# Three of four score blocks split for fp32r, six buffers for rows of scores, and a small copy moved to ScalarE

## The chip, the core and the metric

The kernel runs on one core of a Trainium2 chip. The metric is the device time of one execution in microseconds (us); the kernel before took 876.58 us (median of 3 runs, 874.64 to 881.66). The engines are named as the profile names them: PE (TensorE matmul) with PEld (its weight loads), DVE (VectorE), ACT (ScalarE), POOL (GpSimd), and SP, whose queue issues nearly all DMAs.

## What is computed

Attention with a mixing of the 12 heads ahead of the softmax and another behind it, then a two-matrix layer with a quadratic gate. The sizes are batch 4, 12 heads, 448 positions, 64 columns per head; 1792 tokens of 768, inner width 2048.

```python
scores = scale * q @ k.T
scores = einsum('bhij,hg->bgij', scores, w_pre)    # "first mixing"
attn = softmax(scores)
attn = einsum('bhij,hg->bgij', attn, w_post)       # "second mixing"
x = (attn @ v)  -> [1792, 768]
h = x @ w_in;  g = where(h >= 1, h, where(h <= -1, 0, (h + 1)**2 / 4))
out = g @ w_out
```

## The kernel before

The attention part takes about the first 430 us after a short start, the layer the rest. A *tile* is up to 120 query rows of one batch entry (three tiles of 120 and one of 88 per entry, 16 in all). Scores of a tile are made for all 12 heads and kept in SBUF as `ssb`, 120 rows by 12 heads by 448. For the first mixing heads and rows must lie together on the partitions, so `load_s` (L198) copies ten rows of `ssb`, with their twelve heads, by DMA into a buffer `s10` of 120 partitions by 448: that is a *block*. A tile of 120 rows has 12 blocks, one of 88 rows has 9; there are 180. A tile's blocks make three *groups* of 4 (or of 3), 48 groups in all.

The order of work is written out by hand: one *window* per group n in the main loop (from L880 on), and every engine runs its instructions in that order. In window n the program has

- on SP's queue, first the loads of s for group n+1 (L198), then loads of q, k, v and of layer weights, and stores;
- on PE `pre(m)` for the blocks 0, 1, 2, 3 of group n in that order (L217 or L219), transposes of q and k for a later tile, the products with v (`pv`, L302 and L307, into `ps_q`), the second mixing of group n-1 (L272, L256), and at the window's end a third of the scores of a later tile (`scores`, L180, the first half into the same `ps_q`, of which there is one);
- on DVE the row maxima of the four blocks (L222), one split of a block of group n+1 (L206, L207), a reciprocal (L235), low parts of transposed k and q (L146, L166), part of the copy of `pv`'s product into `xo` (L326), the other split, two steps of a weight conversion (L373, L374, in windows that have one), and the copy of the scores into `ssb` (L183);
- on ACT the exponentials (L228), then the copies of `pv` (L319) and of the second mixing (L258), and half of the scores (L185).

`pre` has two forms. A block that was *split* into a high and a low fp32r part (`split`, L201 to L208) is mixed by three matmuls (L217); one that was not is mixed in fp32 (L219), which the trace shows as two records per block. Before the change the blocks 1 and 3 of each group but the first are split (block 1 of a group of 3): 82 of 180. Their loads are issued first, so the order of loads is 1, 3, 0, 2. `s10` has 8 buffers, the high and low parts 2 each.

For a tile of 88 rows the copy into `xo` has a second piece of 2 by 18 columns (`full < nb`, L322 to L328): DVE does it for three of the four such tiles (9 copies), ACT for the last.

The first group of a tile can be loaded only after the last third of that tile's scores was copied into `ssb` (L183, L185), which happens two windows before the group is used. The convert-and-store of layer weights and the loads of v run in the same SP queue between the loads of s.

Of the kernel before, what the change touches and what calls it, by code (L numbers as in the profile page):

```python
# [9 lines left out]
F32 = mybir.dt.float32  # L10
F32R = mybir.dt.float32r
# [3 lines left out]
AF = mybir.ActivationFunctionType  # L15
# [7 lines left out]
def tile_talking_heads_moe(  # L23
# [11 lines left out]
    nc = tc.nc  # L35
    B, H, S, D = q.shape
# [5 lines left out]
    KM = IB * H  # L42
# [16 lines left out]
    ap_ = s_att.enter_context(tc.tile_pool(name="att", bufs=2))  # L59
# [14 lines left out]
    tiles = []  # L74
    for b in range(B):
        for i0 in range(0, S, QT):
            n = min(QT, S - i0)
            tiles.append((b, i0, n, -(-n // IB)))
    blocks = []
    groups = []  # L80
# [6 lines left out]
    NG = len(groups)  # L87
# [99 lines left out]
    s10 = {}  # L187
# [6 lines left out]
    def load_s(m):  # L194
        t, o, ni, c = blocks[m]
        n, nb = tiles[t][2:]
        x = ap_.tile([KM, S], F32, tag="s10", name="s10", bufs=8)
        nc.sync.dma_start(out=x[:ni * H], in_=ssb[t][o:n:nb])  # L198
        s10[m] = x

    def split(m):  # L201
        k = blocks[m][2] * H
        x = s10.pop(m)
        hi = ap_.tile([KM, S], F32R, tag="sh", name="sh", bufs=2)
        lo = ap_.tile([KM, S], F32R, tag="sl", name="sl", bufs=2)
        nc.vector.tensor_copy(out=hi[:k], in_=x[:k])  # L206
        nc.vector.tensor_tensor(out=lo[:k], in0=x[:k], in1=hi[:k].bitcast(F32), op=ALU.subtract)  # L207
        s10[m] = (hi, lo)  # L208

    def pre(m):  # L210

        k = blocks[m][2] * H
        lps[m] = ps_l.tile([KM, S], F32, tag="l", name="ps_l")
        x = s10.pop(m)
        if isinstance(x, tuple):
            for j, (w, y) in enumerate(((wpre_h, x[0]), (wpre_l, x[0]), (wpre_h, x[1]))):
                nc.tensor.matmul(out=lps[m], lhsT=w[:k], rhs=y[:k], start=(j == 0), stop=(j == 2))  # L217
        else:
            nc.tensor.matmul(out=lps[m], lhsT=wpre[:k], rhs=x[:k], start=True, stop=True)  # L219

    def row_max(m, nm):
        nc.vector.tensor_reduce(out=nm, in_=lps[m], axis=AX.X, op=ALU.max, negate=True)  # L222
        lps[m] = (lps[m], nm)
# [24 lines left out]
    def post(m):  # L248
        t, o, ni, c = blocks[m]
        a = place(t)[0]  # L250
        ps = ps_l.tile([128, KC, H * IB], F32, tag="l", name="ps_a")
        e, w = ex[m], wr[m]
        for r in range(KC):
            for s in ((0, 1), (1, 0))[r % 2]:
                c0 = r * 128 + s * 64
                nc.tensor.matmul(out=ps[half[s], r, :ni * H], lhsT=e[:, c0:c0 + 64], rhs=w[:, :, :ni],  # L256
                                 start=True, stop=True)
        nc.scalar.activation(out=a[:, :, :, c:c + ni],  # L258
                             in_=ps[:, :, :ni * H].rearrange("q r (h i) -> q r h i", h=H), func=AF.Copy)
# [23 lines left out]
    def banks_x(n):  # L283
        if n < NG - 4:
            x = pair()
        elif n < NG:
            x = bank(0)
        else:
            return [ps_l.tile([128, QT], F32, tag="l", name="ps_x") for m in range(2)]
        return [x[:, :, :QT]]  # L290

    def pv(t, g, step):
        b, i0, n, nb = tiles[t]
        if g == 0:
            xo[t] = ap_.tile([128, HP, QT], F32, tag="xo", name="xo", bufs=2)
        ps = banks_x(step)
        to = [ps[0][:, m, :] for m in range(2)] if len(ps) == 1 else ps
        a, ar = aT[t]
        x, xr = vt[b, g]
        for s in range(2):  # L300
            for m, p in enumerate(half):
                nc.tensor.matmul(out=to[m][half[s], :n], lhsT=xr[p, s, :], rhs=ar[p, 2 * g + s, :n],  # L302
                                 start=True, stop=False)
        for m in range(2):
            for r in range(KC):
                for s in ((0, 1), (1, 0))[r % 2]:
                    nc.tensor.matmul(out=to[m][half[s], :n], lhsT=x[:, 2 * m + s, r * D:(r + 1) * D],  # L307
                                     rhs=a[:, r, 4 * g + 2 * m + s, :n], start=False, stop=(r == KC - 1))

        full = n - (IB - 1) * nb  # L310

        def out():
            for i, p in enumerate(ps):
                to = xo[t][:, 2 * g:2 * g + 2, :nb * IB]
                if len(ps) == 2:
                    to = to[:, i:i + 1]
                    p = p.unsqueeze(1)
                to = to.rearrange("p m (a o) -> p m a o", o=nb)
                nc.scalar.activation(out=to[:, :, :, :full],  # L319
                                     in_=p[:, :, :full * IB].rearrange("p m (o a) -> p m a o", a=IB),  # L320
                                     func=AF.Copy)
                if full < nb:  # L322
                    x = to[:, :, :IB - 1, full:]
                    y = p[:, :, full * IB:n].rearrange("p m (o a) -> p m a o", a=IB - 1)
                    if t + 1 < len(tiles):
                        nc.vector.tensor_copy(out=x, in_=y)  # L326
                    else:
                        nc.scalar.activation(out=x, in_=y, func=AF.Copy)  # L328
        return out

    def visit(n, rests):
        v = [lambda x=x: pv(*x, n) for x in vis2.pop(n, ())]
        if rests:
            v.insert(len(v) if n < NE else 0, lambda: post_rest(rests))
        return [f() for f in v]
# [46 lines left out]
    def conv(n, f):  # L382
        if n in CS and CS.index(n) < 2 * NF:
            f(CS.index(n))
# [372 lines left out]
    with tc.manual_schedule():  # L757
# [45 lines left out]
        for m in groups[0]:  # L803
# [7 lines left out]
            out=wpre.rearrange("p (i g) -> p i g", g=H),  # L811
# [3 lines left out]
            out=wpost, in0=wrep[:, 1, :].unsqueeze(2).to_broadcast([KM, H, IB]),  # L815
# [59 lines left out]
        def w0_lo():  # L875
            wts[0] = wts[0]()
            sum_x("B11", "B12", "B11", 0)
            sum_x("B12", "B22", "B12", 0)
# [11 lines left out]
        for n in range(NG + 2):  # L890
            if n == NE:
                s_qk.close()
                s_se.close()
                pool['w'] = ctx.enter_context(tc.tile_pool(name="ffw", bufs=2, side="right",
                                                           reuse_waits="tile"))
                pool['ps_h'] = ctx.enter_context(tc.tile_pool(
                    name="ps_h", bufs=1, space=PSUM, side="right", reuse_waits="tile"))
            if n == NG - 1:
                s_ss.close()
            ms = groups[n] if n < NG else ()  # L900
            old = list(groups[n - 1]) if 0 < n <= NG else []
            if n + 1 < NG:
                for m in (*groups[n + 1][1::2], *groups[n + 1][::2]):
                    load_s(m)
            for f in loads.get(n, ()):
                f()
            if ms:
                sm = ap_.tile([KM, 4], F32, tag="sm", name="sm", bufs=3)
                nm = ap_.tile([KM, 4], F32, tag="nm", name="nm", bufs=3)
            for m in ms:  # L910
                pre(m)
            nxt = list(groups[n + 1][1::2]) if n + 1 < NG else []
            turned = [f() for f in [f() for f in at.pop(n, ())]]
            for f in mid.pop(n, ()):
                f()
            conv(n + 1, conv_load)
            for m in ms:
                row_max(m, nm[:, m - ms[0]:m - ms[0] + 1])
            if n == NG - 1:
                w0_lo()  # L920
            if nxt:
                split(nxt.pop(0))
            rests = list(old)
            early = n < NE
            copies = visit(n, rests) if early else ()
            for j, m in enumerate(ms):
                if j == 3 and old and not early:
                    post(old.pop(0))
                exps(m, j, sm)
            conv(n, conv_scaled)  # L930
            if ms:
                norm(ms, sm)
            for f in (*turned, *copies):
                f()
            for m in nxt:
                split(m)
            if n == NG:
                step(0)
            for m in old:
                post(m)  # L940
            conv(n, conv_rest)
            conv(n - 1, conv_store)
            if not early:
                for f in visit(n, rests):
                    f()
            for t, hps in vis.pop(n, ()):
                scores(t, hps)
            for f in late.pop(n, ()):
                f()
# [155 lines left out]
```

## Time and profile before

| | us | share of the span |
|---|---|---|
| median of three runs | 876.58 (874.64 to 881.66) | |
| the profiled execution, device time | 878.23 | |
| its span in the profile | 876.5 | |
| PE busy | 854.6 | 97% |
| DVE busy | 644.6 | 74% |
| ACT busy | 563.5 | 64% |
| POOL busy | 213.9 | 24% |
| chain that ended last: PE | | 84% |
| chain that ended last: DMA | | 9% |

The profiled execution lies 1.7 us over its span and 1.65 us over the median. "Busy" of PE is modelled from starts, so idle PE is read from gaps and waits more safely than from the busy share. A wait is put down to what ended last. DMA share is the mean busy share of the core's 16 DMA engines.

### The profile page before, as it was taken

Reading aid. Unit: us, or ns where it says so; the run is one execution under the profiler, and the core shown is the slowest. Engines: PE = TensorE matmul, PEld = TensorE weight load, DVE = VectorE, ACT = ScalarE, POOL = GpSimd, SP = SyncE. Lnnn points to the kernel's source line nnn. Section 1 sums busy time; section 2 is a strip of 40 time slices with the busy share of each in tenths; the row PEclk is TensorE's granted clock in tenths of the full one; section 3 lists DMA queues with packets and bytes.
Section 4 is the critical chain, followed back from the end, with each engine's and each line's share of the span. In section 5 each row is a group of like instructions: output and inputs, shape, how many; then the busy total and the mean of one; then the engine's idle time right before and its main releaser. Section 6 shows DMA issues by size and latency. Waiting matters only on the chain.

```text
span 876.5 us, 19947 instructions
## 1 busy us (share of the span) xinstructions
PE 854.6 (97%) x7850; PEld 736.4 (84%) x7850; DVE 644.6 (74%) x945; ACT 563.5 (64%) x1162; POOL 213.9 (24%) x269
## 2 busy tenths in 40 slices
PE   8999999999998999989999999999999999999998
PEld 6678877778776778768778788899999999999998
DVE  3888577786766776867668877997668978777853
ACT  3688788787886778868776566676667534433431
POOL 0266235663355543656320000000000000000000
PEclk8999999999999999999999999999999999999999
DMA  7687769986699876988555745654444444123331
GB/s 160 209 239 236 207 186 264 267 257 196 170 255 253 249 210 172 278 261 260 180 182 169 265 150 172 224 189 133 129 116 162 154 171 135 55 84 115 107 128 63
DMA packets 155329, 162.47 MB, mean 185 GB/s; under 512 B 66916, under 2 KB 148964, under 8 KB 155236
## 3 DMA queue, kind: packets, MB, share of 16 engines
q1 hardware_dynamic: 152404, 160.51, 60.9%
q8 instruction: 62, 1.02, 0.5%
q10 hardware_dynamic: 2832, 0.69, 0.4%
q14 instruction: 31, 0.25, 0.1%
HBM read 88.81 MB, written 33.82 MB: 140 GB/s over the span
## 4 chain that ended last, share of the span: by engine, by line
PE 84%; DMA 9%; DVE 3%; ACT 2%; SPq 1%; issue 1%; ACTq 0%
PE ps_f L711 23%; PE ps_f L546 21%; PE ps_a L256 10%; PE ps_l L219 8%; PE ps_q L307 5%; PE ps_l L217 5%; DMA s<-ssb 4%; PE ps_q L180 3%; PE ps_s L180 3%; DMA v<-in_v_dram 2%; PE ps_r L272 2%; PE ps_q L302 1%; DMA k<-in_k_dram 1%; PE ps_k L141 1%; DMA wraw<-in_moe_w_in_dram 1%; PE ps_t L161 1%
## 5 line engine op out<-in xcount | busy, mean ns | idle before, releaser
L239 POOL TENSOR_SCALAR wr<-wpost,rs 120x120 f32<-120x120 f32 x180 | 142.1, 805 | 64.0 <-DVE rs L235 47.4
L228 ACT ACTIVATE e<-ps_l,nm 120x448 f32<-120x448 f32 x180 | 112.1, 631 | 55.6 <-DVE nm L222 54.5
L256 PE MATMUL ps_a<-wr,e 120*64 120x120 f32 (+1 forms) x2160 | 118.9, 266 | 0.0
L222 DVE TENSOR_REDUCE nm<-ps_l 120x1 f32<-120x448 f32 x180 | 105.0, 619 | 13.6 <-PE ps_l L219 10.4
L256 PEld LDWEIGHTS ps_a<-wr,e 120*64 120x64 f32 x2160 | 110.2, 137 | 2.6 <-issue 2.6
L694 ACT ACTIVATE sgh_p<-gq_p 128x1024 fp32r<-128x1024 f32 (+1 forms) x56 | 53.3, 953 | 90.5 <-PE ps_f L711 90.3
L438 DVE SCALAR_TENSOR_TENSOR wl<-wi,wh 128x768 fp32r<-128x768 f32 x71 | 67.7, 954 | 41.9 <-ACT wh L435 41.3
L711 PE MATMUL ps_f<-wh,sgh_p 128*128 128x384 f32 x294 | 98.2, 334 | 0.0
L711 PE MATMUL ps_f<-wh,sgl_p 128*128 128x384 f32 x294 | 98.2, 334 | 0.0
L711 PE MATMUL ps_f<-wl,sgh_p 128*128 128x384 f32 x294 | 98.2, 334 | 0.0
L435 ACT ACTIVATE wh<-wi 128x768 fp32r<-128x768 f32 x71 | 59.7, 842 | 58.7 <-DVE wi L658 18.0
L219 PE MATMUL ps_l<-s,wpre 120*120 120x448 f32 x196 | 93.7, 562 | 1.9 <-ACT ssb L185 1.1
L258 ACT ACTIVATE aT<-ps_a 128x360 f32<-128x360 f32 x180 | 79.9, 493 | 13.3 <-PE ps_a L256 4.7
L695 DVE TENSOR_TENSOR sgl_p<-gq_p,sgh_p 128x1024 fp32r<-128x1024 f32 (+1 forms) x56 | 60.9, 1089 | 35.7 <-ACT sgh_p L694 35.7
L206 DVE CAST sh<-s 120x448 fp32r<-120x448 f32 (+1 forms) x82 | 32.5, 396 | 59.4 <-DMA s<-ssb 59.4
L183 DVE COPY ssb<-ps_q 120x896 f32<-120x896 f32 (+1 forms) x48 | 52.1, 1085 | 29.6 <-PE ps_q L180 29.6
L185 ACT ACTIVATE ssb<-ps_s 120x448 f32<-120x448 f32 (+1 forms) x96 | 47.1, 544 | 28.7 <-PE ps_s L180 26.6
L376 POOL TENSOR_TENSOR wt<-wt,wk 128x768 int32<-128x768 int32 x32 | 58.2, 1820 | 6.7 <-ACT wk L372 6.7
L217 PE MATMUL ps_l<-sh,wpre_h 120*120 120x448 f32 (+1 forms) x82 | 58.7, 715 | 0.0
L711 PEld LDWEIGHTS ps_f<-wh,sgh_p 128*128 128x128 f32 x294 | 55.2, 188 | 0.0
L711 PEld LDWEIGHTS ps_f<-wl,sgh_p 128*128 128x128 f32 x294 | 55.2, 188 | 0.0
L711 PEld LDWEIGHTS ps_f<-wh,sgl_p 128*128 128x128 f32 x294 | 55.2, 188 | 0.0
(234 smaller groups left out, 1946.3 us busy)
## 6 DMA issues: line engine op xcount, KB each, us to landing
s<-ssb SPq DMA_DIRECT2D x172, 210.0 KB
wraw<-in_moe_w_in_dram SPq DMA_DIRECT2D x16, 768.0 KB
wraw<-in_moe_w_out_dram SPq DMA_DIRECT2D x16, 768.0 KB
wi<-wod SPq DMA_DIRECT2D x29, 384.0 KB
wi<-wsd SPq DMA_DIRECT2D x28, 384.0 KB
wsd<-wt SPq DMA_DIRECT2D x16, 384.0 KB
wod<-wt SPq DMA_DIRECT2D x16, 384.0 KB
wi<-wss SPq DMA_DIRECT2D x16, 384.0 KB
```

The costliest lines, as they stand in the source:

```text
L217: nc.tensor.matmul(out=lps[m], lhsT=w[:k], rhs=y[:k], start=(j == 0), stop=(j == 2))
L219: nc.tensor.matmul(out=lps[m], lhsT=wpre[:k], rhs=x[:k], start=True, stop=True)
L222: nc.vector.tensor_reduce(out=nm, in_=lps[m], axis=AX.X, op=ALU.max, negate=True)
L228: nc.scalar.activation(out=e, in_=ps, func=AF.Exp, bias=nm, accum_out=sm[:, j:j + 1])
L239: nc.gpsimd.tensor_scalar_mul(out=w[:, :, :ni], in0=wpost[:, :, :ni], scalar1=rs[:, j:j + 1])
L256: nc.tensor.matmul(out=ps[half[s], r, :ni * H], lhsT=e[:, c0:c0 + 64], rhs=w[:, :, :ni], start=True, stop=True)
L258: nc.scalar.activation(out=a[:, :, :, c:c + ni], in_=ps[:, :, :ni * H].rearrange("q r (h i) -> q r h i", h=H), func=AF.Copy)
L435: nc.scalar.activation(out=hi, in_=t, func=AF.Copy, scale=2.0 ** -8)
L438: nc.vector.scalar_tensor_tensor(out=lo, in0=t, scalar=2.0 ** -8, in1=hi.bitcast(F32), op0=ALU.mult, op1=ALU.subtract)
L546: nc.tensor.matmul(out=o, lhsT=u[:, c, k], rhs=x, start=first and r == 0 and m == 0, stop=r == 2 and m == 2, skip_group_check=True)
L695: nc.vector.tensor_tensor(out=lo, in0=src, in1=hi.bitcast(F32), op=ALU.subtract)
L711: nc.tensor.matmul(out=o, lhsT=x[:, f, c], rhs=y[:, f % 2, :], start=first and f == 0 and m == 0, stop=hf == 1 and f == 3 and m == 2, skip ...
```

## The change

All blocks of a group but block 0 are split (so 129 instead of 82 of the 180: 47 more, one more in each group but the first). The loads of a group come in the order 1, 2, 3, 0. The buffers for loaded rows go from 8 to 6, those for the high and low parts from 2 to 3 each, so the SBUF they take together is the same. The small second piece of the copy into `xo` is always done by ACT.

```diff
     def load_s(m):
-        x = ap_.tile([KM, S], F32, tag="s10", name="s10", bufs=8)
+        x = ap_.tile([KM, S], F32, tag="s10", name="s10", bufs=6)
     def split(m):
-        hi = ap_.tile([KM, S], F32R, tag="sh", name="sh", bufs=2)
-        lo = ap_.tile([KM, S], F32R, tag="sl", name="sl", bufs=2)
+        hi = ap_.tile([KM, S], F32R, tag="sh", name="sh", bufs=3)
+        lo = ap_.tile([KM, S], F32R, tag="sl", name="sl", bufs=3)
...
                     y = p[:, :, full * IB:n].rearrange("p m (o a) -> p m a o", a=IB - 1)
-                    if t + 1 < len(tiles):
-                        nc.vector.tensor_copy(out=x, in_=y)
-                    else:
-                        nc.scalar.activation(out=x, in_=y, func=AF.Copy)
+                    nc.scalar.activation(out=x, in_=y, func=AF.Copy)
...
             if n + 1 < NG:
-                for m in (*groups[n + 1][1::2], *groups[n + 1][::2]):
+                for m in (*groups[n + 1][1:], groups[n + 1][0]):
                     load_s(m)
...
-            nxt = list(groups[n + 1][1::2]) if n + 1 < NG else []
+            nxt = list(groups[n + 1][1:]) if n + 1 < NG else []
```

## Rows read from the trace of the kernel before

**Rows 1.** The page: busy time by engine, and the chain by engine.
```profile
PE 854.6 (97%) x7850; PEld 736.4 (84%) x7850; DVE 644.6 (74%) x945; ACT 563.5 (64%) x1162; POOL 213.9 (24%) x269
...
PE 84%; DMA 9%; DVE 3%; ACT 2%; SPq 1%; issue 1%; ACTq 0%
```

**Rows 2.** Windows view: start:end, length, busy us (count) by engine, clock, DMA share, GB/s.
```profile
27.30:72.60 45.30, 45.23 (x515) 33.93 (x515) 37.42 (x71) 37.37 (x98) 24.55 (x32) 1.00 0.82 234
72.60:120.00 47.40, 47.40 (x604) 37.57 (x604) 32.78 (x57) 36.65 (x90) 19.05 (x28) 1.00 0.74 208
120.00:192.00 72.00, 69.11 (x921) 54.86 (x921) 54.40 (x102) 57.50 (x144) 41.75 (x45) 1.00 0.87 258
192.00:231.00 39.00, 39.00 (x492) 30.77 (x489) 26.07 (x45) 29.66 (x73) 14.47 (x23) 1.00 0.67 191
231.00:306.00 75.00, 69.69 (x921) 54.71 (x921) 53.06 (x100) 56.53 (x144) 40.76 (x45) 1.00 0.88 246
306.00:345.00 39.00, 39.00 (x490) 30.68 (x486) 26.93 (x47) 29.31 (x73) 15.34 (x23) 1.00 0.69 194
345.00:418.00 73.00, 69.82 (x924) 55.17 (x923) 55.63 (x103) 58.13 (x145) 43.87 (x48) 1.00 0.85 258
418.00:456.00 38.00, 36.97 (x503) 28.59 (x502) 22.92 (x43) 27.31 (x73) 12.50 (x23) 1.00 0.55 183
```

**Rows 3.** Waits of the whole run: us in total, times, longest.
```profile
DVE sh L206 <- DMA s<-ssb: 59.4, 38, 4.4
PE ps_q L180 <- DVE xo L326: 9.5, 6, 2.3
```

**Rows 4.** Timeline of PE, first mixings of one group: start, us, instruction.
```profile
212.86 1.01 PE L219 MATMUL ps_l<-s,wpre 120*120 120x448 f32 x2
...
214.12 0.36 PE L217 MATMUL ps_l<-sl,wpre_h 120*120 120x448 f32 x1
214.32 0.91 PE L219 MATMUL ps_l<-s,wpre 120*120 120x448 f32 x2
```

**Rows 5.** Timeline of PE around 256 to 280.
```profile
266.28 0.46 PE L180 MATMUL ps_q<-kh,qh 64*120 64x448 f32 x2 [2.34 <-DVE xo L326]
267.69 1.01 PE L219 MATMUL ps_l<-s,wpre 120*120 120x448 f32 x2
...
276.45 0.46 PE L180 MATMUL ps_q<-kh,qh 64*120 64x448 f32 x2 [1.47 <-DVE xo L326]
278.28 0.98 PE L219 MATMUL ps_l<-s,wpre 120*120 120x448 f32 x2 [0.34 <-DMA s<-ssb]
```

**Rows 6.** Timeline of DVE around 264 to 280.
```profile
264.56 0.39 DVE L206 CAST sh<-s 120x448 fp32r<-120x448 f32 x1 [4.39 <-DMA s<-ssb]
264.98 0.63 DVE L207 TENSOR_TENSOR sl<-s,sh 120x448 fp32r<-120x448 f32 x1
265.52 0.17 DVE L235 RECIPROCAL rs<-rs 120x4 f32<-120x4 f32 x1
...
268.56 1.08 DVE L183 COPY ssb<-ps_q 120x896 f32<-120x896 f32 x1
...
275.17 0.39 DVE L206 CAST sh<-s 120x448 fp32r<-120x448 f32 x1 [3.41 <-DMA s<-ssb]
...
276.68 0.41 DVE L206 CAST sh<-s 120x448 fp32r<-120x448 f32 x1 [0.28 <-DMA s<-ssb]
```

**Rows 7.** Timeline of SP's queue, loads of s for two successive groups.
```profile
259.23 3.37 SPq L198 DMA_DIRECT2D s<-ssb  x4
...
267.55 4.46 SPq L198 DMA_DIRECT2D s<-ssb  x4
```

**Rows 8.** Chain in order of time, two places: start, us, what.
```profile
269.56 8.59 DMA s<-ssb
278.14 0.14 issue
...
391.14 8.22 DMA s<-ssb
399.36 0.14 issue
```

**Rows 9.** The tile xo: duration ns min/median/max, first and last start.
```profile
L326 DVE COPY xo<-ps_q x9: 170/191/194, 141.8 to 388.2; 128x36 f32<-128x36 f32 x9
L328 ACT ACTIVATE xo<-ps_x x6: 187/198/246, 466.6 to 468.3; 128x18 f32<-128x18 f32 x6
```

**Rows 10.** Windows view of a stretch in which loads of s move nearly alone.
```profile
122.00:125.00 3.00, 3.00 (x68) 2.84 (x66) 2.07 (x6) 2.97 (x9) 0.92 (x3) 1.00 0.65 243
```

**Rows 11.** Timeline of DVE at 192, where a long stretch of conversions ends.
```profile
192.22 1.08 DVE L183 COPY ssb<-ps_q 88x896 f32<-88x896 f32 x1
193.45 2.61 DVE L222 TENSOR_REDUCE nm<-ps_l 120x1 f32<-120x448 f32 x4 [0.15 <-PE ps_l L219]
```

## The prediction

> **What bounds the kernel now.** I read the page first. PE is busy for 854.6 of 876.5 us and carries 84% of the chain that ended last, DMA 9% and DVE 3% [rows 1]. A bound that looks like PE throughout has to be read by stretch, because all of the change lies in the attention part, 27 to 456 us, and because the sum over stretches hides who comes second. The windows view cut at the places where the DMA share changes shows two kinds [rows 2]. In four stretches (27 to 73, 120 to 192, 231 to 306, 345 to 418; 265 us together) the DMA engines are busy for 82 to 88% of the time; three of them are also the ones in which PE stands idle, 2.9, 5.3 and 3.2 us. In the four between (163 us together) the DMA share is 55 to 74% and PE is idle for 1.0 us in all: there PE sets the pace.
>
> Next the waits. PE's largest one in the attention part is the scores (L180) waiting for DVE's small copy of xo (L326): 9.5 us in six times; DVE waits 59.4 us in 38 times for loads of s in its splits [rows 3]. The timelines tie the two together. In the window that begins at 256, the loads of s for the next group are issued at 259.2 [rows 7]; DVE's first split stands until 264.56, 4.39 us idle, for the first of them [rows 6]; behind it on DVE queue the reciprocal, the copy L326 and the rest; PE's scores need the `ps_q` that L326 reads and start at 266.28 after 2.34 us of idleness [rows 5]. The window behind repeats it with 1.47 us. So the wait carries DVE's name, but a transfer is what is late.
>
> Last the chain in order of time, for what sets the beginning of a window inside such a stretch. PE begins the window at 278.28 after 0.34 us of waiting for a load of s [rows 5], and the chain has that load from 269.56 to 278.15 [rows 8]. It is the third of the four issued from 267.55 on [rows 7], and by the old order 1, 3, 0, 2 the third is block 0, the one that PE mixes first. The same pattern stands at 391.14 to 399.36 [rows 8]. The three landings of that group can be read off: 275.15 and 276.66 from DVE's two waiting casts [rows 6], 278.14 from PE. They are 1.5 us apart although three issues lie within 2.9 us: the transfers queue behind one another.
>
> **The change part by part.** *Splits on PE.* One block fewer in fp32, one more in three fp32r matmuls. By the modelled ends of one group's mixings, the fp32 pair ends at 213.87, the fp32r triple behind it at 214.48 and the next fp32 pair at 215.23 [rows 4]: 0.61 us against 0.75, so 0.14 us saved per block. Over 47 blocks this is 6.6 us, if PE set the pace in every window. It does so in the 163 us of the low-DMA stretches. A window takes (456 - 27.3)/48 = 8.9 us on average, so these are about 18 windows and 18 x 0.14 = 2.5 us. In the others the bytes that DMA has to move don't change, and what PE saves is waited for again; I take 0 there, and 4.1 us as the other end.
>
> *The order of loads.* Block 0 becomes the fourth load, and PE still needs it first. Where a window's beginning is held by the third load today, it will be held by the fourth. No row shows when the fourth lands. From below it is 0 (it lands before PE is through with the window anyway, as between the stretches), from above the 1.5 us at which the landings follow each other in rows 5 and 6; the pitch of four unhindered issues, 3.37/4 = 0.84 us [rows 7], lies between. I take 1.0. This doesn't add up from window to window as long as the transfers are what is late, because the landings then stay at their absolute times. It counts once at the end of each of the four stretches, where PE takes over again: 4 x 1.0 = 4.0 us, bounds 0 and 6.0.
>
> *The copy L326.* Moved to ACT it costs about 0.2 us (an ACT copy of half its size 0.198, L326 itself 0.191 on DVE [rows 9]), nine times, 1.8 us on an engine that is idle for 20 to 25% of these stretches [rows 2]; hidden. The six waits of 9.5 us disappear under that name. What is late next is the beginning of the following window: with scores done 2.3 us sooner, PE meets block 0, which is now the last load. At 278 today's order already gives PE only what was left after the wait of 1.47 us, and still a wait of 0.34 us for the third load. So I take 0 of the 9.5 us as kept; the other end is all of it.
>
> *Splits on DVE.* A split takes 0.96 us from its cast to the next instruction (264.56 to 265.52 [rows 6]), so 47 x 0.96 = 45 us more. In a stretch of 72 us with 8 windows DVE goes from 54.4 to 62.1 us, 86% [rows 2]. That fits, but the new split stands ahead of the copy of scores into `ssb` (L183), so this copy and the next row maxima come a split later. At 192, where a stretch of conversions ends, DVE was idle for only 0.15 us ahead of the row maxima [rows 11], so they will be late by up to 0.8 us there and the exponentials on ACT behind them; PE first has the other mixings and transposes to do, which covers about 0.5 of it. I take 0.3 us for each of the three places like this, 0.9 us, bounds 0 and 3 x 0.96 = 2.9. The later L183 also delays the loads of the first group of each tile. In a loaded stretch they queue anyway: at 259.23 they are issued and only at 264.5 does the first land [rows 6, 7]. I take 0.
>
> *The buffers.* The third and fourth load of a group now wait for the first and second split of the group before, the ones that free their buffers. Those splits end at 265.52 and about 267.1 [rows 6]; the third load of the group behind is issued at 269.56 [rows 8]. The buffer is free in time: 0. Where SP runs further ahead (the low-DMA stretches), a load that is held back for a microsecond or two has a whole window left; 0 there too.
>
> The sum: -2.5 + 4.0 + 0 + 0.9 = +2.4 us. Against the profiled execution (878.23, span 876.5) this gives 880.6, and on the median of the three runs 876.58 + 2.4 = 879.0.
>
> A rule and a row about whether the loaded stretches are really full. A DMA share of 85 to 88% [rows 2] reads like 12 to 15% of room, and then loads could land sooner, once engines ask sooner. But in a stretch in which loads of s move nearly alone the share is 0.65 with transfers queued behind each other [rows 10]. The Trainium skill ("DMA: Bandwidth & Descriptors", section "Why a DMA increments its semaphore by 16 and not by 1") says that a copy is spread over the largest number of engines, up to 16, that divides the slowest dimension on both sides. For ten rows of `ssb` into 120 partitions that would be ten of 16, an estimate of 0.63, and the trace's 0.65 agrees. By that rule 0.85 to 0.88 has little room left; by the share alone up to 9 us in the 72 would be free. It is why the first rival below gets no more than its chance.
>
> **The rivals.** *A: the stalls go for good.* If the fourth load lands before PE gets to the next window, the 9.5 us of waits for L326 and the 6.6 us of PE work are both kept: 876.6 - 16.1 = 860.5. With half of the waits kept and the low-DMA splits, about 8 us, it is 868. For it: the waits have DVE's name, and DVE in-order blocking is what the change removes. Against it: the third load already comes too late at 278 and 399 [rows 5, 8], and the fourth comes later. It decides where the fourth load lands within half a microsecond of the third.
>
> *B: the delay feeds itself; slower.* If what is late is the issue of the loads and not their bytes, a window that begins 1 us later copies its scores 1 us later, the next tile's loads start 1 us later, and the shift adds up. About 30 windows lie in the loaded stretches (265/8.9). A shift of 1.0 us kept in a third to a half of them is 10 to 15 us, with 2.5 saved: 884 to 889, and with a split's 0.96 us on DVE in each path up to 893. It decides from the point where the DMA queues run dry between two groups' loads. Against it: the spacing of 1.5 us of landings issued faster than that.
>
> *C: DVE becomes the bound.* 86% busy with waits for PE and DMA between may be full. If every one of some 24 windows with a conversion grows by 0.4 us, this is +10 us: 887. Against it: DVE's idle time is mostly the wait for s itself, 59.4 us [rows 3], which the work can move into.
>
> *D: the time stays and nothing is decided.* The split's saving and the later block 0 cancel to less than a microsecond: 876 to 878. It is the forecast with other roundings and shares its chance.
>
> **How the numbers follow.** About 1% (8.8 us) is what a measurement of this kernel can tell from no change. The forecast with D gets 0.70, its own range being 873 to 884 (the terms at their bounds: -2.5 - 4.1 + 0 at one end, about +6.0 + 2.9 - 2.5 at the other, rounded out by the run-to-run spread). A gets 0.12, B 0.13, C 0.05. Faster by over 1% is A: 0.12. Slower by over 1% is B and C: 0.18. Within 1%: 0.70. For 8 in 10 the range has to reach some way into A and over most of B: 866 to 890.
>
> **What would show it.** If the steps are right: the wait of PE for L326 is gone; in its place PE's first fp32 mixing of a window (L219) waits for loads of s in the loaded stretches, some 10 us in all; the low-DMA stretches are each 0.5 to 0.9 us shorter, the loaded ones about 1 us longer; DVE has 129 splits, 45 us more work, and waits less than 59 us for s. The prediction is wrong if PE has no such wait (then A), if SP waits longer for L183 and the DMA share falls in the loaded stretches (then B), or if PE waits for `ps_q` or for exponentials behind DVE without a load being late (then C).

## The result, and the profile after

The changed kernel took 883.88 us (median of 11 runs, 876.27 to 886.84), the kernel before 877.37 us in the same series (11 runs, 874.64 to 882.28). The ratio is 1.0062 with a 95% interval of 1.0038 to 1.0085: 5.4 us more, 3.3 to 7.5. (The two medians lie 6.5 us apart; the text goes by the ratio and its interval.) That is within 1%, and the sign is settled.

The profiled execution after took 884.98 us with a span of 883.2; that is 6.75 us over the profiled one of before. A profile shows one execution, and executions of one kernel lie several us apart (876.27 to 886.84 here), so the ratios decide and the profiles only explain. Its page, busy time by engine and the chain by engine, as in [rows 1]:

```profile
PE 852.0 (96%) x7897; PEld 747.2 (85%) x7897; DVE 688.1 (78%) x1030; ACT 558.7 (63%) x1171; POOL 218.6 (25%) x269
...
PE 68%; DVE 13%; DMA 10%; ACT 6%; issue 2%; SPq 0%; POOL 0%; ACTq 0%; DVEq 0%
```

DVE does 43.5 us more and is busy for 78% of the span, so nobody would call it the bound. The chain says more: PE's share fell from 84% to 68%, and DVE's rose from 3% to 13%, ACT's from 2% to 6% [rows 1]. DMA rose by one point only. DVE has come into the path that sets the end.

The windows view of after, cut at the beginnings of the same windows of the program as in [rows 2] (which lie later here), in the same columns:

```profile
27.30:75.50 48.20, 44.93 (x521) 34.97 (x520) 41.63 (x81) 36.51 (x97) 23.87 (x32) 1.00 0.73 221
75.50:123.80 48.30, 47.12 (x609) 38.51 (x609) 38.32 (x69) 36.27 (x91) 20.84 (x28) 1.00 0.73 204
123.80:200.30 76.50, 71.33 (x931) 58.15 (x929) 62.58 (x116) 57.80 (x147) 44.07 (x46) 0.96 0.83 246
200.30:238.40 38.10, 38.10 (x492) 31.43 (x491) 29.17 (x53) 29.06 (x73) 14.71 (x22) 1.00 0.66 188
238.40:312.30 73.90, 68.91 (x932) 56.40 (x930) 61.90 (x116) 56.47 (x147) 41.66 (x47) 1.00 0.85 251
312.30:350.30 38.00, 38.00 (x492) 31.42 (x490) 29.07 (x53) 28.86 (x73) 14.51 (x21) 1.00 0.69 196
350.30:424.90 74.60, 68.92 (x932) 56.45 (x930) 61.85 (x116) 55.54 (x147) 41.82 (x46) 1.00 0.82 250
424.90:462.60 37.70, 36.52 (x509) 29.73 (x508) 27.99 (x52) 27.11 (x74) 15.30 (x24) 1.00 0.58 189
```

Against [rows 2] the eight lengths changed by +2.9, +0.9, +4.5, -0.9, -1.1, -1.0, +1.6 and -0.3 us, together +6.6. The loaded stretches (the first, third, fifth and seventh) gave +7.9, but not alike: one of them became shorter. The stretches between gave -1.3. In the loaded stretches the DMA share fell from 0.82, 0.87, 0.88 and 0.85 to 0.73, 0.83, 0.85 and 0.82. In the third and seventh this is what the same bytes give over a longer time (0.87 x 72 / 76.5 = 0.82, 0.85 x 73 / 74.6 = 0.83); in the first and fifth it is lower than that.

Waits of the whole run after (us in total, times, longest), then those of SP's queue between 27 and 470 us:

```profile
ACT e L228 <- DVE nm L222: 81.3, 50, 4.2
...
DVE sh L206 <- DMA s<-ssb: 32.0, 32, 2.9
...
PE ps_l L219 <- DMA s<-ssb: 13.0, 11, 2.9
```

```profile
SPq L198 <- DVE ssb L183: 74.8, 24, 11.1
SPq L198 <- DVE sh L206: 12.8, 15, 2.5
```

PE's wait for the small copy into `xo` (9.5 us in [rows 3]) is gone; its wait of 13.0 us for a load of s stands in its place. DVE waits 27 us less for loads; part of the third split's work now fills that idleness. Two waits have grown that [rows 3] doesn't show: before, ACT's exponentials waited 54.5 us for row maxima, and SP waited 59.8 us for L183 (the copy of scores into `ssb`). Now they wait 81.3 and 74.8 us.

### The profile page after: what moved, and what is told of

Read it like the earlier page. It is cut to its first block, busy times and chain, and to the rows that moved or that the text cites. A ratio compares the mean times of both kernels' runs of the same rounds, so it can differ in the third digit from the quotient of the medians.

```text
span 883.2 us, 20160 instructions
## 1 busy us (share of the span) xinstructions
PE 852.0 (96%) x7897; PEld 747.2 (85%) x7897; DVE 688.1 (78%) x1030; ACT 558.7 (63%) x1171; POOL 218.6 (25%) x269
## 3 DMA queue, kind: packets, MB, share of 16 engines
q1 hardware_dynamic: 152404, 160.51, 59.8%
## 4 chain that ended last, share of the span: by engine, by line
PE 68%; DVE 13%; DMA 10%; ACT 6%; issue 2%; SPq 0%; POOL 0%; ACTq 0%; DVEq 0%
PE ps_f L708 23%; PE ps_f L543 21%; DMA s<-ssb 8%; PE ps_a L256 6%; PE ps_l L217 4%; ACT e L228 3%; PE ps_l L219 3%; PE ps_q L307 3%; DVE ssb L183 2%; PE ps_q L180 2%; DVE wt L371 2%; DVE sl L207 2%; DVE sh L206 2%; PE ps_s L180 2%; DVE wt L370 1%
## 5 line engine op out<-in xcount | busy, mean ns | idle before, releaser
L228 ACT ACTIVATE e<-ps_l,nm 120x448 f32<-120x448 f32 x180 | 112.0, 632 | 81.8 <-DVE nm L222 81.3
L239 POOL TENSOR_SCALAR wr<-wpost,rs 120x120 f32<-120x120 f32 x180 | 146.6, 830 | 37.3 <-DVE rs L235 30.8
L222 DVE TENSOR_REDUCE nm<-ps_l 120x1 f32<-120x448 f32 x180 | 103.1, 617 | 9.1 <-PE ps_l L219 7.7
L207 DVE TENSOR_TENSOR sl<-s,sh 120x448 fp32r<-120x448 f32 x129 | 82.0, 636 | 4.4
L206 DVE CAST sh<-s 120x448 fp32r<-120x448 f32 x129 | 52.0, 403 | 32.6 <-DMA s<-ssb 32.0
L219 PE MATMUL ps_l<-s,wpre 120*120 120x448 f32 x102 | 51.2, 589 | 17.0 <-DMA s<-ssb 13.0
L183 DVE COPY ssb<-ps_q 120x896 f32<-120x896 f32 (+1 forms) x48 | 52.1, 1085 | 17.0 <-PE ps_q L180 16.9
L217 PE MATMUL ps_l<-sh,wpre_h 120*120 120x448 f32 x129 | 64.4, 499 | 0.0
L185 ACT ACTIVATE ssb<-ps_s 120x448 f32<-120x448 f32 (+1 forms) x96 | 48.1, 569 | 16.5 <-PE ps_s L180 15.3
L234 POOL TENSOR_SCALAR rs<-sm 120x4 f32<-120x4 f32 (+1 forms) x48 | 12.6, 262 | 177.0 <-ACT e L228 177.0
```

What stands on the lines that cost most here:

```text
L183: nc.vector.tensor_copy(out=ssb[t][:n, h:h + 2, :], in_=wide[:n, :, :S])
L228: nc.scalar.activation(out=e, in_=ps, func=AF.Exp, bias=nm, accum_out=sm[:, j:j + 1])
L239: nc.gpsimd.tensor_scalar_mul(out=w[:, :, :ni], in0=wpost[:, :, :ni], scalar1=rs[:, j:j + 1])
```

## Experiments

Each kernel was measured beside runs of the kernel before. Where "on before" or "on after" stands, the edit was made to that kernel. "Before" had medians of 879.52, 875.92 and 876.1 us in the three series.

**The parts, one by one.** First the copy alone, on before:

```diff
-                    if t + 1 < len(tiles):
-                        nc.vector.tensor_copy(out=x, in_=y)
-                    else:
-                        nc.scalar.activation(out=x, in_=y, func=AF.Copy)
+                    nc.scalar.activation(out=x, in_=y, func=AF.Copy)
```

> The kernel before with one part of the change: the small second piece of xo is copied by ScalarE in all tiles. Late-block theory (the transfers of s set when a window can begin, so a wait taken from TensorE comes back as another): within 2 us of the kernel before, the 9.5 us of waits of L180 for xo gone from the list, and in their place waits of the first mixing for loads of s. Rival (the stalls go for good): 6 to 10 us faster.

Measured 874.5 us, ratio 0.9963 (0.9933 to 0.9993): 3.2 us less, 0.6 to 5.9. This lies between the two expectations: with two splits in a window, about a third of the 9.5 us is kept. PE's waits of this kernel show where the rest went:

```profile
PE ps_s L180 <- DVE ql L166: 4.0, 4, 1.6
PE ps_l L219 <- DMA s<-ssb: 3.1, 3, 1.4
```

The wait for `xo` is gone. Behind the same late split now stands the low part of q (`ql`), which PE's scores need too, and behind that the load of block 0.

Then the buffers alone, on before (`s10` 8 to 6, `sh` and `sl` 2 to 3):

```diff
-        x = ap_.tile([KM, S], F32, tag="s10", name="s10", bufs=8)
+        x = ap_.tile([KM, S], F32, tag="s10", name="s10", bufs=6)
...
-        hi = ap_.tile([KM, S], F32R, tag="sh", name="sh", bufs=2)
-        lo = ap_.tile([KM, S], F32R, tag="sl", name="sl", bufs=2)
+        hi = ap_.tile([KM, S], F32R, tag="sh", name="sh", bufs=3)
+        lo = ap_.tile([KM, S], F32R, tag="sl", name="sl", bufs=3)
```

> The kernel before with the buffers of the change alone: six for rows of s, three each for the high and low parts; splits and order of loads as before. Both theories: no effect by themselves, within 2 us. If the loads lose because SP has to wait for a buffer: slower by 3 us or more, and SP's waits for the splits (L207) grow.

Measured 876.81 us, ratio 0.9985 (0.9954 to 1.0016): no effect clear of the noise with two splits. With three splits SP does wait for them before it can load again (12.8 us for L206, above); what those waits cost wasn't tried, since there is no room for eight `s10` beside three parts each.

Then the order of loads alone, on before, as 1, 3, 2, 0:

```diff
-                for m in (*groups[n + 1][1::2], *groups[n + 1][::2]):
+                for m in (*groups[n + 1][1::2], *groups[n + 1][2::2], groups[n + 1][0]):
```

> The kernel before with the order of loads 1, 3, 2, 0 in place of 1, 3, 0, 2: block 0 lands last, no split is added. Late-block theory: TensorE's first mixing waits for loads of s, 4 us slower (2 to 6). Late-copy theory (what costs is the added split on VectorE ahead of the copy of scores L183, which delays the next tile's loads): within 1.5 us of the kernel before.

Measured 881.42 us, ratio 1.0037 (1.0010 to 1.0064): 3.2 us more, 0.9 to 5.6, as the late-block theory had it. PE's waits:

```profile
PE ps_l L219 <- DMA s<-ssb: 6.7, 11, 1.7
PE ps_q L180 <- DVE xo L326: 4.2, 5, 1.9
```

Both stalls are there side by side, together 10.9 us where before had 9.5 of the second.

And the copy put back on DVE, on after (the first diff of this section in reverse):

> The changed kernel with the small second piece of xo copied by VectorE again. Late-copy theory: the copy again stands behind a split that waits for a load, as in the kernel before, so the scores wait for it; 2 to 5 us slower than the changed kernel, 1.008 to 1.012 of the kernel before. If the stall only changes its name, as the prediction had it: like the changed kernel, 1.004 to 1.008.

Measured 880.84 us, ratio 1.0052 (1.0030 to 1.0073), the same as after within its interval. PE's waits:

```profile
PE ps_l L219 <- DMA s<-ssb: 6.8, 8, 1.7
PE ps_q L180 <- DVE xo L326: 5.7, 5, 2.0
```

Their sum is 12.5 us; after has 13.0 in the first alone. So with the third split and block 0 last, where the copy runs decides little but the name of the wait. The 3.2 us that the copy gives alone don't show inside the change.

**What the third split costs on DVE.** On before, one of the two splits is done twice, with the same result, so that DVE has a split's work more ahead of L183; no other instruction is added or moved. (The eight added lines shift the line numbers: L236 is the exponential, L230 the row maximum.)

```diff
+    def again():
+        x, hi, lo, k = last[0]
+        nc.vector.tensor_copy(out=hi[:k], in_=x[:k])
+        nc.vector.tensor_tensor(out=lo[:k], in0=x[:k], in1=hi[:k].bitcast(F32), op=ALU.subtract)
...
+            if n + 1 < NG:
+                again()
             for m in nxt:
                 split(m)
```

> The kernel before with one split of each group done twice on VectorE (same values written again), just ahead of the second split; nothing else changes: same matmuls, loads, buffers. It puts 0.97 us per window ahead of the copy of scores L183. Late-copy theory (VectorE's added work ahead of L183 delays the next tile's loads and the exponentials, and this feeds itself in the loaded stretches): 6 to 10 us slower, 1.007 to 1.012. Late-block theory (the cost is that block 0 lands last): within 1.5 us of the kernel before.

Measured 881.88 us, ratio 1.0059 (1.0031 to 1.0086): 5.2 us more, 2.7 to 7.5. This is the clearest of the runs: no load was reordered, no matmul changed, and the loss is as large as that of the whole change. The chain by engine and the waits:

```profile
PE 73%; DMA 10%; DVE 9%; ACT 4%; issue 2%; SPq 1%; POOL 0%; ACTq 0%; DVEq 0%; POOLq 0%
```

```profile
ACT e L236 <- DVE nm L230: 78.0, 48, 3.7
...
DVE sh L206 <- DMA s<-ssb: 37.2, 27, 3.1
```

DVE's share of the chain is 9%, against 3% in the kernel before and in the two that only move the copy or the loads. DVE's wait for loads fell by 22 us (from 59.4), and its wait for PE's scores ahead of L183 by another 14 (from 29.4 to 15.3). So most of the 45 us of added work (47 x 0.96) went into idle time; what didn't fit made DVE late, and ACT waits for row maxima 24 us more.

**Where on DVE's queue it hurts.** On after, the two conversion steps, with the ACT and GpSimd steps of the same function, are put behind the copy L183, which then has 1.5 us less of work ahead of it in windows that have them:

```diff
-            conv(n, conv_rest)
             conv(n - 1, conv_store)
...
             for t, hps in vis.pop(n, ()):
                 scores(t, hps)
+            conv(n, conv_rest)
```

> The changed kernel with the weight conversion's second half (two VectorE steps, 1.5 us, and what hangs on them) behind the scores and their copy L183 instead of ahead. L183 comes up to 1.5 us sooner, the row maxima behind it come when they came. If the added split costs by delaying the next tile's loads: 0.998 to 1.002 of the kernel before. If it costs by delaying the row maxima and so the exponentials: 1.004 to 1.010, as changed.

Measured 879.33 us, ratio 1.0031 (1.0006 to 1.0056). This lies between the two expectations. In the profiled run PE's wait for loads is 5.0 us (13.0 in after), SP's for L183 55.9 (74.8), ACT's for row maxima 67.2 (81.3). But this execution took 875.31 us, 4.0 less than its kernel's median, and the one of after 1.1 more than its own, so a part of these differences lies between executions and not in the edit. By the medians and ratios about half of the loss is back (2.7 of 5.4 us); the intervals of the two kernels overlap, so even that is not settled. Since the row maxima stand behind the conversion in both, what this order brings forward is L183 and the loads that it triggers; but ACT's wait shrank as well, so the two paths are not told apart by it.

The same move on before with the copy on ACT, two splits in a window (the two diffs are those above):

> The kernel before with the copy of xo on ScalarE and the conversion's second half behind the copy L183. If late loads are what the loaded stretches lose to: 0.990 to 0.994. If the exponentials: 0.994 to 1.000, like the ScalarE copy alone or worse.

Measured 877.88 us, ratio 1.0016 (0.9984 to 1.0048): nothing gained over the copy alone, and by the ratio itself above both expected ranges, though SP's wait for L183 fell (50.1 us; 57.3 with the copy alone). So with two splits an earlier L183 bought no time here.

The other direction, on after: the conversion's DVE steps ahead of the first split of a window, where DVE waits for loads.

```diff
-            if nxt:
-                split(nxt.pop(0))
...
+            conv(n, conv_mid)
+            if nxt:
+                split(nxt.pop(0))
             if ms:
                 norm(ms, sm)
```

(`conv_mid` is the two steps, taken out of `conv_rest`.)

> The changed kernel with VectorE's two steps of the weight conversion (1.5 us per window that has one) moved from behind the last split to ahead of the first, where VectorE waits for loads of s. Late-copy theory: L183 comes up to 1.5 us sooner in loaded stretches, and the whole loss goes: 0.995 to 1.001 of the kernel before. Late-block theory: TensorE still waits for block 0, 1.004 to 1.008.

Measured 894.62 us, ratio 1.0212 (1.0179 to 1.0244), which neither theory had. The waits say why:

```profile
ACT e L228 <- DVE nm L222: 93.3, 49, 3.1
...
DVE wt L368 <- ACT wt L362: 58.5, 32, 2.1
```

The conversion needs a step of ACT (L362) that stands behind the exponentials, and these wait for DVE's row maxima. So DVE now waits for ACT, which waits for DVE, and the splits stand behind. The move made a loop; it doesn't test what it was meant to. The same on before with the copy on ACT:

> The kernel before (two splits, old order of loads, eight buffers) with the copy of xo on ScalarE and the conversion's VectorE steps ahead of the first split. Late-copy theory: L183 sooner than in the kernel before, the waits for loads in the loaded stretches shrink: 0.990 to 0.995. If bytes bound these stretches: like the ScalarE copy alone, 0.993 to 0.999.

Measured 880.2 us, ratio 1.0053 (1.0030 to 1.0077), with DVE waiting 54.9 us for L362: the same fault, less costly with two splits.

**Other places for the third split and for block 0.** On after, block 0 third and block 3 last:

```diff
-                for m in (*groups[n + 1][1:], groups[n + 1][0]):
+                for m in (*groups[n + 1][1:3], groups[n + 1][0], *groups[n + 1][3:]):
```

> The changed kernel with the order of loads 1, 2, 0, 3: block 0 lands third as in the kernel before, and block 3, the last to be split, lands last. Late-block theory: the waits of the first mixing for loads of s (13 us) mostly go, and the time falls by 4 us or more against the changed kernel, to 0.998 to 1.002 of the kernel before. Late-copy theory: the copy L183 stays late, and the time stays at 1.004 to 1.008.

Measured 891.63 us, ratio 1.0180 (1.0137 to 1.0222): much slower. PE's largest wait, in an execution of 898.0 us:

```profile
PE ps_q L302 <- DVE ssb L183: 15.6, 16, 2.0
```

The wait for block 0 is all but gone (one of 2.6 us), yet the third split now needs the last load, and L183 stands behind that split. PE can't write `ps_q` again before L183 has read it. So the order of loads in the change is the better of the two: DVE's in-order queue needs the loads sooner than PE does.

On after, the last split of each group on GpSimd:

```diff
-                split(m)
+                split(m, nc.gpsimd if m == groups[n + 1][-1] else nc.vector)
```

> The changed kernel with the last split of each group done by GpSimd instead of VectorE; all else as changed (129 blocks in fp32r, block 0 last, six buffers). VectorE's work is that of the kernel before. Late-copy theory: the loss goes, 0.996 to 1.002 of the kernel before, unless GpSimd is late in its turn. Late-block theory: TensorE still waits for block 0, 1.004 to 1.008.

Measured 881.53 us, ratio 1.0059 (1.0032 to 1.0086): no better than after. (One added line: L208 is the subtraction.) SP's queue waits for the new split:

```profile
SPq L198 <- POOL sl L208: 21.6, 14, 4.9
```

SP's wait for L183 is back where it was (52.4 us; 59.8 before), but GpSimd's split takes 0.55 + 1.15 us where DVE's takes 0.39 + 0.63, holds its `s10` buffer, and so delays the next loads (21.6 us) and PE (5.5 us). One late engine was exchanged for another, and block 0 stays the last load (PE waits 8.8 us for it).

On before with the copy on ACT and the changed buffers, a third split only in the 19 windows in which PE was taken to set the pace:

```diff
+            if n + 1 < NG and n > 1 and (n not in CS or len(groups[n]) == 3):
+                nxt += groups[n + 1][2:3]
```

> The kernel before with the copy of xo on ScalarE, the buffers of the change, the old order of loads, and a further split only in 19 windows: those without a weight conversion (but the first two) and those of groups of three. Both theories say that TensorE sets the pace there: 19 x 0.14 = 2.6 us less than the ScalarE copy alone, 0.990 to 0.995 of the kernel before.

Measured 876.34 us, ratio 1.0003 (0.9983 to 1.0024). The expectation failed: 19 x 0.14 = 2.7 us saved on PE and the 3.2 of the copy should have shown. The trace shows a part of the reason. Fifteen windows are 0.12 to 0.15 us shorter than in the trace of the copy alone, 2.0 us together. But in the order of loads 1, 3, 0, 2 the added split takes the last load, as in the kernel with block 0 third, and six of the windows chosen also have a conversion. In one of these, from 340.7 us on, DVE's third split waits for its load:

```profile
349.12 0.39 DVE L206 CAST sh<-s 120x448 fp32r<-120x448 f32 x1 [0.37 <-DMA s<-ssb]
```

L183 stands behind it and starts at 351.59, 3.1 us behind the beginning of the next window (0.1 with the copy alone), and that window takes 9.84 us instead of 8.17. Loaded windows differ by up to 2 us between the two traces, so this isn't the whole account. No version tried beat the copy alone.

## Why the prediction held, and where its steps did not

The forecast of +2.4 us stands against +5.4 (3.3 to 7.5): within 1%, inside the range, on the right side, but low. The hit owes something to luck: the range was wide enough for a term that came out several times its size. (The own range of the forecast has a slip at its lower end, too: -2.5 - 4.1 from 876.6 is 870, not 873. It had no part in the outcome.) By its steps:

**Splits on PE: right where PE sets the pace, but less in all.** Two PE-set windows follow each other in the second stretch. PE's first mixings of them, before and then after:

```profile
91.70 1.01 PE L219 MATMUL ps_l<-s,wpre 120*120 120x448 f32 x2
...
101.94 1.01 PE L219 MATMUL ps_l<-s,wpre 120*120 120x448 f32 x2
```

```profile
95.87 1.01 PE L219 MATMUL ps_l<-s,wpre 120*120 120x448 f32 x2
...
105.96 1.01 PE L219 MATMUL ps_l<-s,wpre 120*120 120x448 f32 x2
```

The window took 10.24 us and takes 10.09: 0.15 saved where 0.14 was worked out from [rows 4]. Where PE sets the pace this repeats window after window. Of the stretches between, three shrank by 0.9, 1.0 and 0.3 us, where 0.5 to 0.9 was forecast. The second stretch alone grew (+0.9), because its first window takes 9.89 us instead of 8.98, with PE waiting 0.88 us for block 0 at its end. So the four gave 1.3 us, where 2.5 was forecast.

**The order of loads: right.** The cleanest place is the second window, before anything has shifted. PE's first mixing there, before and after:

```profile
31.98 0.98 PE L219 MATMUL ps_l<-s,wpre 120*120 120x448 f32 x2
```

```profile
33.52 0.98 PE L219 MATMUL ps_l<-s,wpre 120*120 120x448 f32 x2 [1.55 <-DMA s<-ssb]
```

The four loads land at 30.1, 31.0, 31.8 and 33.4 us in both kernels. Block 0 was the third and is the fourth, and PE starts 1.54 us later: the upper bound that the prediction took from landings 1.5 us apart [rows 5, 6]. That is more than the 1.0 it settled on. The order alone costs 3.2 us (0.9 to 5.6) where the term was 4.0, and PE's 13.0 us of waits for loads answer to "some 10 us in all". The loaded stretches did not grow by about 1 us each, though: +2.9, +4.5, -1.1 and +1.6 us hold the third split's cost as well, and the clock.

**The copy on ACT: right for the change, wrong by itself.** An ACT copy takes 0.24 us (0.2 forecast from [rows 9]). Inside the change its stall only changed its name, as was said; alone the copy kept 3.2 us (0.6 to 5.9), which no bound of the forecast's own range had.

**The buffers: 0 alone, as forecast.** Beside three splits it stays open.

**The third split on DVE: the term that was mis-sized.** The prediction put 0.9 us on it, for row maxima late at three places, and 0 on the loads behind a late L183. One repeated split costs 5.2 us (2.7 to 7.5), where 2.9 was the upper bound. Two places of the chain show how it works. The first stretch was counted as one that loads hold, by its DMA share of 0.82; but PE is busy there for 45.23 of 45.30 us [rows 2], and before, the chain followed back from 73 us to 37 is PE alone (start, us, what):

```profile
59.49 2.46 PE ps_a L256 x48
...
63.36 0.94 PE ps_l L219 x2
```

After, followed back from 76 us to 33, it has no transfer either. It goes round between DVE and ACT, of which this is a turn:

```profile
59.11 1.00 DVE ssb L183
60.12 0.54 DVE nm L222
...
60.68 2.57 ACT e L228 x8
63.26 0.80 ACT wt L362
64.05 0.29 ACT qh L165
...
64.37 0.43 DVE ql L166
...
68.22 1.00 DVE ssb L183
```

The row maxima stand behind the copy L183 on DVE, the exponentials wait for the row maxima, and behind the exponentials on ACT stand a conversion step (L362) and the high part of a transposed q (L165). DVE's low part of q (L166) waits for that, and behind it on DVE stand the second and third split, the conversion and the next L183. One split more makes the round longer: the four windows from 39.45 on take 36.1 us, where the same four took 34.4 before. In the repeat run the chain from 36.2 to 56.4 us is likewise DVE and ACT alone. So the row maxima were late in window after window here, and not at three places where a long stretch of conversions ends.

In the third stretch transfers take part. After, then the queue's own line, then before, in the same windows of the program:

```profile
151.01 1.01 DVE ssb L183
...
152.07 3.80 DMA s<-ssb
...
160.90 1.00 DVE ssb L183
...
162.86 7.62 DMA s<-ssb
```

```profile
160.18 3.45 SPq L198 DMA_DIRECT2D s<-ssb  x4
```

```profile
155.69 6.44 DMA s<-ssb
...
162.15 0.41 DVE sh L206
...
165.00 0.98 PE ps_l L219 x2
```

The first copy releases loads: it ends 2.8 us behind the window's beginning at 149.2, where it ended 1.1 us behind that at 144.3, and SP starts the loads at 152.07. Yet the window is no longer for it: 9.82 us, where it took 10.48. The second copy releases none, though the chain names it. The four loads of that window start at 160.18, ahead of its end, and the one at 162.86 is the last of them, block 0, issued directly behind the others. They start 1.2 us behind the window's beginning at 159.0 (before, 0.9 behind 154.8). This window takes 11.62 us, where it took 10.21, and 0.8 of the difference is the order's: from the landing that DVE's first split waits for to PE's start are 3.67 us (166.95 to 170.62), where it was 2.85 (162.15 to 165.00), because PE needs the fourth load and not the third. In the fifth and seventh stretch loads of s are 41 and 28% of the chain, with DVE and ACT between them.

The prediction saw that L183 comes later, and took the loads to queue anyway because in one window [rows 6, 7] they did; in the window just read that is not far off. Its larger fault was to ask if DVE's 86% leaves room, when the question was what stands behind the added work on an in-order queue, and what waits for that on ACT's. This mixes rivals B and C. By the prediction's own words B holds if SP waits longer for L183 and the DMA share falls in the loaded stretches, and both came (59.8 to 74.8 us, and all four shares). C's sign, PE waiting for exponentials behind DVE without a late load, is there in the first stretch, though with 0.9 us it is small. Each came at a price below the one that its rival had, because most of the split's work still fits into DVE's idle time. How much of the 5.2 us goes by the loads and how much by the exponentials isn't settled for the other stretches.

With these sizes the parts add to about the measured time: -2.5 on PE (the forecast's figure), +3.2 for the order, +5.2 for the split and 0 for the copy are +5.9, against +5.4; with the 1.3 that the stretches between gave they are +7.1. The intervals of two of them are several us wide, so both agree but prove little. A share of the loss may also go with TensorE's clock (last section), which the prediction didn't have at all.

## What to carry to other kernels

Ask of added work not how full its engine is, but what stands behind it on that engine's queue: here a split of 0.96 us per window, ahead of a copy and of row maxima that loads and exponentials wait for, cost 5.2 us, where the matmul time to be saved was put at 2.5. When a wait bears one engine's name and a late transfer lies beneath it, moving the named instruction changes the name. An order of loads has two customers, and each is in-order: count for both what the last load holds up before choosing which block comes last. And a high DMA share doesn't tell that a stretch waits for DMA: in the first one it was 0.82 with PE idle for 0.07 us.

## What the runs showed of the hardware

In [rows 2] the granted clock is 1.00 throughout, from 27 to 456 us; the third stretch after has 0.96. Behind the 2.88 us that PE waited for the load that lands at 170.5, matmuls of one kind (L217) take 0.57 us, where [rows 4] have 0.36 (the first column of the timeline is the start):

```profile
170.62 1.82 PE L219 MATMUL ps_l<-s,wpre 120*120 120x448 f32 x2 [2.88 <-DMA s<-ssb]
...
172.61 0.57 PE L217 MATMUL ps_l<-sh,wpre_l 120*120 120x448 f32 x1
```

The windows view gives the granted clock (the column ahead of the DMA share):

```profile
170.60:175.00 4.40, 4.38 (x10) 3.16 (x11) 3.87 (x7) 1.30 (x4) 3.77 (x3) 0.50 0.78 247
...
182.00:186.00 4.00, 4.00 (x32) 2.79 (x30) 3.65 (x6) 3.26 (x9) 1.82 (x1) 1.00 0.22 72
```

That is half speed, 1.2 GHz. The window that begins there took 11.82 us where it took 9.20 before, without a wait of PE in it, so some 2.6 of the 4.5 us of its stretch are the clock. The Trainium skill ("TensorE: Matmul & The Clock Gate", section "HAM oscillation — how this bites in real kernels") describes this course, a wait for DMA after which the work behind it starts at the low clock, and in that the trace agrees. So a wait that a change lengthens can be paid twice.

Over whole executions, the changed kernel's mean granted clock was 0.993 in 11 runs; in the later series the kernel before had 0.996. In the runs of each kernel the time goes with that clock, by 0.45 to 0.97 us for each 0.001. By that an estimate of 1.4 to 2.9 of the 5.4 us goes with the clock; that the order of work lowers it by its waits is likely from the place just shown, but not tested. The mean of a whole execution doesn't tell where the clock was low. Before, in the profiled run, that was ahead of the attention part, at the start; the profiled run of the repeated split has full clock there, and low clock at two places within:

```profile
12.70:19.40 6.70, 6.70 (x29) 4.61 (x30) 3.59 (x5) 3.30 (x7) 0.00 (x0) 0.50 0.69 166
```

```profile
157.90:161.20 3.30, 3.30 (x8) 1.87 (x7) 3.27 (x6) 0.90 (x3) 3.30 (x3) 0.50 1.05 362
...
383.20:386.50 3.30, 3.30 (x12) 1.79 (x9) 3.23 (x6) 0.98 (x2) 3.30 (x4) 0.50 1.09 302
```

So although the repeated split has the same mean clock as before (0.996), it isn't shown that its 5.2 us are of order alone.
